# Chunk 0's q and k through two hardware queues, short dummy matmuls, and a new order of the opening

## The chip, the core and the metric

The kernel runs on one core of a Trainium2 chip. The metric is the device time of one execution in microseconds (us), lower is better. The core has five engines that work at the same time and wait for each other by semaphores: TensorE (PE; PEld is its weight load), VectorE (DVE), ScalarE (ACT), GpSimd (POOL) and SyncE (SP). Sixteen DMA engines move data between memory (HBM) and the on-chip buffer (SBUF). Matmul results go to eight PSUM banks, named ps0 to ps7.

## The reference

The kernel computes causal sliding-window attention and passes its result through a gated feed-forward block:

```python
# q, k, v: (8, 8, 576, 64) float32; w_gate, w_val: (512, 1536); w_out: (1536, 512)
scores = q @ k.transpose(0, 1, 3, 2) / 8.0
mask = (rel >= 0) & (rel < 64)              # rel = query position - key position
attn = softmax(where(mask, scores, -1e9))
x = (attn @ v).transpose(0, 2, 1, 3).reshape(4608, 512)
g = x @ w_gate
out = (g * sigmoid(g) * (x @ w_val)) @ w_out    # (4608, 512) float32
```

## The kernel before

The 4608 tokens are cut into 36 chunks of 128 for the attention, and into 9 blocks of 512 (four chunks each) for the feed-forward part. All matmuls are in bf16. Loads from HBM convert float32 to bf16 on their way, and these all are issued by POOL, in one order. SP issues the output DMAs and, for later chunks, DMA transposes.

One chunk n goes through these steps, which are the words of the two tables LOADS and STEPS:

- `kq:n` loads q and k (tiles qn, kn), `v:n` loads v (tile va), `ld:n` does both. `w:a:b` loads columns a to b (in units of 128) of both gate and value weights (Wg, Wv); `wo:a:b` loads rows of the output weights (Wo).
- `TQ:n`, `TK:n` transpose q and k on PE (L293); `qa`, `qd`, `ka`, `kd` move the result from PSUM to qT and kT, on ACT (letter a) or DVE (letter d). `TD:n` does both transposes by DMA on SP instead (L351, L354).
- `S:n` makes the scores on PE (L382), 24 matmuls, and their exponential on ACT (L392, tile pt). It needs kT of chunks n and n-1. Masking is either `M:n`, a multiplication on DVE (L398), or, where `B:n` came before (chunks 0, 2, 3), a bias that PE adds first (L362).
- `A0:n` and `A1:n` are the two halves of pt times v on PE (L432). `N:n` divides by the row sums on DVE (L451, L454, tile xb). `X:n` transposes the result on PE (L529), `xa:n` or `xd:n` moves it to xT; `XD:n` does it by DMA.
- `F:c:f:t0:t1` is one of the 12 parts of the gate and value products of block c, for the columns t0 to t1 (L563): eight matmuls and a tanh on ACT. `U` is the rest of the oldest F on DVE (L572, L574), which writes hT. `O:c:u` is the output product for one chunk (L596), 12 matmuls, a copy on ACT and an output DMA on SP.

The two tables are the order in which every engine gets its instructions: each engine works through its own in that order and waits where data or a buffer is not there yet. Tables cover blocks 0 and 1, most of the attention of chunks 0 to 11, and the scores of 12 and 13. From `F:2:0` on, loops in `build` give the order: per block, 12 F and the four O of the block before, with a pair of chunks placed in the middle of an O (L495, L382). The first such pair is 12, placed in the second O of that loop; it holds `S:14` and `S:15`.

`init` makes constants on DVE: zeros for dummy matmuls (wz), the identity, the masks, and the ones beside v. `warm:10` issues ten dummy matmuls of 512 columns (L318) before any data is there. A PSUM bank goes to the next user that asks, the one that was free longest.

POOL's semaphores come in 16 lanes: a load waits until the 16th load before it has landed. A load into qn or kn also waits until the chunk eight before it has been transposed.

Of the kernel before, what the change touches and what calls it, by code (L numbers as in the profile page):

```python
# [7 lines left out]
B, H, S, D = 8, 8, 576, 64  # L8
DM, DFF = H * D, 1536
T = B * S  # L10
# [8 lines left out]
F32 = dt.float32  # L19
# [130 lines left out]
class _Kernel:  # L150
# [7 lines left out]
    NS = 4  # L158
    NO = 4
    LAST = NFC  # L160
    LOADS = """
    init kq:0 kq:1 kq:2 v:1 v:0 kq:3 v:2 v:3 w:5:7 w:0:2 w:3:5 kq:4 w:7:8 kq:5 v:4 w:2:3 w:10:12 kq:6 w:9:10
    v:6 v:5 w:8:9 kq:7 v:7
    """
    STEPS = """
    warm:10 B:0 TQ:0 qa:0 TK:0 ld:8 ka:0 S:0 TQ:1 TK:1 ld:9 wo:6:12 qd:1 kd:1 TQ:2 qa:2 S:1 TK:2 B:2 kd:2 M:1
    S:2 A0:0 A0:1 A1:0 A1:1 ld:10 N:0 TQ:3 B:3 qa:3 N:1 X:0 TK:3 xa:0 A0:2 ka:3 A1:2 ld:11 wo:0:6 S:3 N:2 X:1
    xd:1 X:2 A0:3 xa:2 A1:3 F:0:5:0:384 N:3 X:3 U F:0:6:0:384 xd:3 F:0:0:0:384 U F:0:1 U U F:0:3 U F:0:4 U
    F:0:7 U TK:4 TQ:4 ld:12 ka:4 TK:5 TQ:5 F:0:0:384:512 qd:4 F:0:5:384:512 U ka:5 S:4 U F:0:2 qd:5 M:4
    F:0:6:384:512 U A0:4 S:5 A1:4 ld:13 U F:0:10 N:4 F:0:11 U M:5 X:4 F:0:9 U xd:4 TK:6 A0:5 U ka:6 A1:5 F:0:8  # L170
    N:5 U X:5 TQ:6 ld:14 xa:5 TQ:7 TK:7 qa:6 F:1:0:0:256 kd:7 qd:7 S:6 F:1:1:0:256 U TQ:8 TK:8 M:6 F:1:2:0:256
    U A0:6 ka:8 U S:7 A1:6 ld:15 TQ:9 N:6 F:1:3:0:256 TK:9 qa:8 U X:6 F:1:4:0:256 xd:6 F:1:5:0:256 U
    F:1:6:0:384 U M:7 ka:9 F:1:7:0:384 U qa:9 A0:7 U S:8 A1:7 ld:16 TQ:10 F:1:8:0:384 N:7 U qa:10 X:7 TK:10
    xa:7 F:1:9:0:384 M:8 ka:10 A0:8 U TD:11 S:9 A1:8 ld:17 F:1:10 N:8 M:9 F:1:11 XD:8 U U A0:9 S:10 A1:9
    F:1:0:256:512 N:9 F:1:1:256:512 U F:1:2:256:512 XD:9 U O:0:0 U M:10 A0:10 S:11 A1:10 O:0:3 N:10 M:11 X:10
    A0:11 xd:10 A1:11 TK:13 N:11 TD:12 TQ:13 ka:13 F:1:3:256:512 qd:13 X:11 F:1:4:256:512 U F:1:5:256:512 U
    TD:14 F:1:6:384:512 U F:1:7:384:512 F:1:8:384:512 U O:0:1 U U xd:11 O:0:2 S:12 S:13 F:1:9:384:512 TD:15
    M:12 U M:13
    """

    def __init__(self, nc, q, k, v, wg, wv, wo, out):
# [5 lines left out]
    def alloc(self):  # L187
        nc = self.nc

        def sb(name, n, dtype=BF):  # L190
            return nc.alloc_sbuf_tensor(name, [128, n], dtype)

        def ring(name, cnt, n, dtype=BF):
            return [sb("%s%d" % (name, i), n, dtype) for i in range(cnt)]

        self.ident = sb("ident", 128)
        self.mask = sb("mask", 128)
        self.Wg = sb("Wg", NK * DFF)[:, :].rearrange("p (c f) -> p c f", c=NK)
        self.Wv = sb("Wv", NK * DFF)[:, :].rearrange("p (c f) -> p c f", c=NK)
        self.Wo = sb("Wo", NF * DM)[:, :].rearrange("p (c m) -> p c m", c=NF)  # L200
        hd = lambda t: t[:, :].rearrange("p (h d) -> p h d", h=H)
        self.qn = [hd(t) for t in ring("qn", self.NQ, DM)]
        self.kn = [hd(t) for t in ring("kn", self.NQ, DM)]
        self.vall = sb("va", self.NV * H * 80)
        va = self.vall[:, :].rearrange("p (i h d) -> p i h d", i=self.NV, h=H)
        self.va = [va[:, i] for i in range(self.NV)]
        self.kT = sb("kT", 4 * (T + 64))[:, :].rearrange("p (c t) -> p c t", c=4)
        self.qa = sb("qT", self.NZ * 4 * 128)[:, :].rearrange("p (c r t) -> p c r t", r=self.NZ, c=4)
        self.qT = [self.qa[:, :, r, :] for r in range(self.NZ)]
        self.one, self.fi, self.df = [sb(x, 128, F32) for x in ("one", "fi", "df")]  # L210
        self.pi = sb("pi", 32, F32)
        self.nmask = sb("nmask", 128)
        self.wz = sb("wz", 512)
        self.pt = [t[:, :].rearrange("p (h x) -> p h x", h=H) for t in ring("pt", self.NP, H * 128)]
        self.rc = ring("rc", 4, 4, F32)
        self.xp = [t[:, :].rearrange("p (j m) -> p j m", j=2) for t in ring("xb", 2, 2 * DM)]
        self.xb = [self.xp[i // 2][:, i % 2] for i in range(4)]
        self.rp = [t[:, :].rearrange("p (j h) -> p j h", j=2) for t in ring("rp", 2, 2 * H, F32)]
        self.xT = [t[:, :].rearrange("p (c t) -> p c t", c=NK) for t in ring("xT", self.NX, NK * 512)]
        self.sig = ring("sig", self.NS, 512)  # L220
        self.uu = ring("uu", self.NS, 512)
        self.hT = [t[:, :].rearrange("p (f t) -> p f t", f=NF) for t in ring("hT", self.NH, NF * 512)]
        self.ost = ring("ost", self.NO, DM, F32)
        self.wup = sb("wup", 1, F32)
        self.ps = [nc.alloc_psum_tensor("ps%d" % i, [128, 512], F32) for i in range(8)]
        self.n_s = 0
        self.pool = {i: i - 8 for i in range(8)}
        self.tb, self.bb, self.ab, self.a1, self.mk, self.glus = {}, {}, {}, {}, {}, []
# [42 lines left out]
    def load_qk(self, n):  # L271
        i = n % self.NQ
        for dst, src, nm in ((self.qn[i], self.q, "qn"), (self.kn[i], self.k, "kn")):
            parts = list(self.segs(128 * n, 128))
            for j, (r, b, s, L) in enumerate(parts):
# [2 lines left out]
                d = dst[r:r + L]  # L278
                self.g.op("pool", lambda e, d=d, a=a: e.dma_start(d, a), writes=ks, dma=True)  # L279

    def move(self, eng, d, a, rk, wk):
        if eng == "act":
            self.g.op("act", lambda e: e.activation(d, a, ACTF.Copy), reads=rk, writes=wk)
        else:
            self.g.op("dve", lambda e: e.tensor_copy(d, a), reads=rk, writes=wk)

    def transposes(self, key, job, reads):
        bank, bk = self.bank()
        tb = bank[:, 0:256].bitcast(BF).rearrange("p (c t) -> p c t", c=4)

        def pe(e):
            for i, a in enumerate(job):
                r = e.transpose(tb[:, i, :], a, self.ident[:, :])  # L293
            return r

        self.g.op("pe", pe, reads=["ident"] + reads, writes=[bk])
        self.tb[key] = tb, bk

    def T(self, which, n):
        t, nm = (self.kn, "kn") if which == "k" else (self.qn, "qn")  # L300
        iq = n % self.NQ
        self.transposes((which, n), [t[iq][:, 2 * c:2 * c + 2, :] for c in range(4)], [(nm, iq, j) for j in range(2)])
# [10 lines left out]
    def warm(self, count):  # L313
        bank, bk = self.ps[7], ("ps", 7)

        def pe(e):
            for _ in range(count):
                r = e.matmul(bank[:, :], self.wz[:, 0:128], self.wz[:, :], start=True, stop=True)  # L318
            return r

        self.g.op("pe", pe, reads=["wz"], writes=[bk])
# [314 lines left out]
    def build(self):  # L636
        W = lambda a, b: (self.load_w("g", a, b), self.load_w("v", a, b))

        def load(n):
# [2 lines left out]
                self.load_v(n)  # L642

        acts = {
            "init": self.init, "v": self.load_v, "w": W, "kq": self.load_qk,
            "wo": self.load_wo, "ld": load,
            "warm": self.warm, "TK": lambda n: self.T("k", n), "TQ": lambda n: self.T("q", n),
            "kd": lambda n: self.ev("k", n, "dve"), "ka": lambda n: self.ev("k", n, "act"),
            "qd": lambda n: self.ev("q", n, "dve"), "qa": lambda n: self.ev("q", n, "act"),
            "B": lambda n: self.bb.__setitem__(n, self.bias(n)),  # L650
# [4 lines left out]
        }  # L655
        for t in (self.LOADS + self.STEPS).split():
            name, *args = t.split(":")
# [15 lines left out]
        pairs = {(2, 1): 12, (2, 2): 14}  # L673
        for n in range(16, NCH, 2):
            pairs[(n - 4) // 4, n % 4] = n
        for c in range(2, self.LAST):
            for u in range(4):
                last = c == NFC - 1 and u == 3
                masks = []
                for s in range(3):  # L680
# [5 lines left out]
                    if s == 1 and not last:  # L686
                        n = pairs.get((c, u))
# [54 lines left out]
```

## Time and profile before

| | us |
|---|---|
| median of 5 runs (lowest to highest) | 336.88 (335.87 to 338.06) |
| the profiled execution, whole time | 336.88 |
| its span, first to last instruction | 335.0 |
| PE busy | 320.6 (96% of the span) |
| DVE busy | 218.0 (65%) |
| ACT busy | 137.4 (41%) |
| POOL busy | 114.5 (34%) |
| first load issued by POOL | 1.25 |
| scores of chunk 0 (S:0) start on PE | 7.53 |
| first F matmul starts | 18.68 |
| first matmul of F:2:0 | 88.94 |

The page cuts the span into 40 slices of 8.4 us. PEclk is the clock that TensorE was granted, in tenths. A row of the chain says from when and for how long the run's last instruction depended on what; "issue" is time in which the engine waited for nothing that the profile shows. Busy PE time includes overlap between matmuls, so the start times of groups are the better clock of its progress.

### The profile page before, as it was taken

How to read it: one execution, taken by the hardware profiler on the slowest of the kernel's cores; microseconds unless marked ns; L12 is line 12 of the kernel's file. 1: busy time of each engine (PE TensorE's matmuls, PEld its weight loads, DVE VectorE, ACT ScalarE, POOL GpSimd, SP SyncE). 2: the span in 40 equal slices, each digit the busy share in tenths (PEclk: the TensorE clock that was granted, in tenths of full speed). 3: DMA queues.
4: the chain of work that ended last, by engine and by line, in shares of the span. 5: the costliest groups of instructions: out<-in, count | busy, mean ns of one | idle time of the engine just before them, and what ended most of it. 6: DMA issues, size and time to landing. Idle time of an engine off the chain costs nothing.

```text
span 335.0 us, 8316 instructions
## 1 busy us (share of the span) xinstructions
PE 320.6 (96%) x3492; PEld 167.0 (50%) x3528; DVE 218.0 (65%) x460; ACT 137.4 (41%) x252; POOL 114.5 (34%) x142
## 2 busy tenths in 40 slices
PE   7799999799899999999999999999999999999997
PEld 3455577467445545454545454545454544444444
DVE  5658999777367766666666666666666666555520
ACT  3634567443525434343525252525252532223222
POOL 8999999590506706050515150100000000000000
PEclk9979999999999999999999999999999999999999
DMA  9999999999999996979696969450506120200012
GB/s 79 157 185 174 166 176 176 159 155 187 174 154 106 142 203 46 158 94 159 94 150 102 180 73 197 51 141 21 139 18 135 25 78 18 78 33 31 32 52 106
DMA packets 168293, 38.56 MB, mean 115 GB/s; under 512 B 157760, under 2 KB 163776, under 8 KB 168256
## 3 DMA queue, kind: packets, MB, share of 16 engines
q0 software_dynamic: 122528, 18.88, 83.2%
q1 hardware_dynamic: 45584, 19.08, 28.7%
q8 instruction: 28, 0.46, 0.5%
q10 hardware_dynamic: 144, 0.07, 0.1%
q14 instruction: 9, 0.07, 0.1%
HBM read 37.75 MB, written 9.44 MB: 141 GB/s over the span
## 4 chain that ended last, share of the span: by engine, by line
PE 86%; DMA 7%; issue 2%; POOL 2%; ACT 1%; DVE 1%; SPq 0%; POOLq 0%
PE ps L563 54%; PE ps L596 24%; DMA va<-in_v_dram 5%; PE ps L382 3%; DMA qT<-qn 3%; PE ps L495 2%; PE ps L432 1%; PE ps L293 1%; POOL qn L279 1%; PE ps L626 1%; POOL kn L279 1%; PE ps L529 1%; SPq L351 0%; ACT pt L392 0%; DVE xb L454 0%
## 5 line engine op out<-in xcount | busy, mean ns | idle before, releaser
L572 DVE SCALAR_TENSOR_TENSOR uu<-sig,ps 128x512 bf16<-128x512 bf16 (+3 forms) x121 | 76.0, 628 | 62.9 <-ACT sig L569 62.4
L563 PE MATMUL ps<-xT,Wv 128*128 128x512 bf16 (+3 forms) x482 | 113.7, 358 | 0.1
L563 PE MATMUL ps<-xT,Wg 128*128 128x512 bf16 (+3 forms) x466 | 110.2, 358 | 1.4 <-issue 0.5
L569 ACT ACTIVATE sig<-ps 128x512 bf16<-128x512 f32 (+3 forms) x121 | 66.7, 552 | 91.9 <-PE ps L563 91.8
L596 PE MATMUL ps<-Wo,hT 128*128 128x512 bf16 x404 | 94.4, 379 | 2.2 <-issue 1.9
L574 DVE SCALAR_TENSOR_TENSOR hT<-uu,ps 128x512 bf16<-128x512 bf16 (+3 forms) x121 | 76.2, 630 | 4.4 <-PE ps L563 0.3
L563 PEld LDWEIGHTS ps<-xT,Wv 128*128 128x128 bf16 x484 | 46.7, 98 | 47.7 <-issue 0.7
L563 PEld LDWEIGHTS ps<-xT,Wg 128*128 128x128 bf16 x484 | 45.7, 98 | 47.8 <-ACT pt L392 1.9
L332 POOL DMA_DIRECT2D va<-in_v_dram x40 | 38.9, 1006 | 82.4 <-PE ps L495 81.3
L596 PEld LDWEIGHTS ps<-Wo,hT 128*128 128x128 bf16 x420 | 40.0, 98 | 46.6
L392 ACT ACTIVATE pt<-ps 128x512 bf16<-128x512 f32 x72 | 37.8, 601 | 26.7 <-PE ps L382 26.5
L608 ACT ACTIVATE ost<-ps 128x512 f32<-128x512 f32 x35 | 20.9, 597 | 66.5 <-PE ps L596 66.4
L279 POOL DMA_DIRECT2D qn<-in_q_dram x40 | 39.1, 996 | 16.4 <-DMA qT<-qn 13.1
L279 POOL DMA_DIRECT2D kn<-in_k_dram x40 | 39.2, 1001 | 0.6 <-DMA qn<-in_q_dram 0.6
L398 DVE TENSOR_TENSOR pt<-pt,mask 128x512 bf16<-128x512 bf16 x66 | 24.3, 419 | 6.3 <-ACT pt L392 6.1
L517 DVE TENSOR_TENSOR xb<-ps,rp 128x448 bf16<-128x448 f32 (+1 forms) x36 | 18.5, 514 | 1.2
L382 PE MATMUL ps<-qT,kT 64*64 64x64 bf16 (+1 forms) x864 | 16.2, 203 | 2.7 <-DMA qT<-qn 1.1
L382 PEld LDWEIGHTS ps<-qT,kT 64*64 64x64 bf16 x864 | 12.5, 108 | 9.2 <-DVE hT L574 4.2
L514 DVE RECIPROCAL rp<-ps 128x7 f32<-128x7 f32 (+1 forms) x36 | 6.7, 187 | 15.4 <-PE ps L495 15.4
L495 PE MATMUL ps<-va,pt 64*64 64x65 bf16 x728 | 11.5, 193 | 0.1
L454 DVE TENSOR_TENSOR xb<-ps,rc 128x256 bf16<-128x256 f32 x24 | 10.2, 425 | 0.8
L432 PE MATMUL ps<-va,pt 64*64 64x65 bf16 x360 | 7.4, 196 | 2.9 <-issue 1.6
(44 smaller groups left out, 97.8 us busy)
## 6 DMA issues: line engine op xcount, KB each, us to landing
out_dram<-ost SPq DMA_DIRECT2D x35, 256.0 KB, 3.3
qn<-in_q_dram POOLq DMA_DIRECT2D x32, 128.0 KB, 7.9
kn<-in_k_dram POOLq DMA_DIRECT2D x32, 128.0 KB, 8.2
va<-in_v_dram POOLq DMA_DIRECT2D x32, 128.0 KB, 7.7
Wo<-in_moe_w_out_dram POOLq DMA_DIRECT2D x2, 768.0 KB, 13.4
Wg<-in_moe_w_gate_dram POOLq DMA_DIRECT2D x4, 256.0 KB, 7.5
Wv<-in_moe_w_val_dram POOLq DMA_DIRECT2D x4, 256.0 KB, 8.1
qn<-in_q_dram POOLq DMA_DIRECT2D x8, 64.0 KB, 7.3
```

Source lines behind the costliest of these rows:

```text
L279: self.g.op("pool", lambda e, d=d, a=a: e.dma_start(d, a), writes=ks, dma=True)
L332: g.op("pool", lambda e, d=d, a=a: e.dma_start(d, a), writes=ks, dma=True)
L382: r = e.matmul(sv[h][o:o + 64, c, q0:q1], self.kT[ps, c, kk:kk + 64], qT[ps, c, q0:q1], start=not biased, stop=not biased or c == 3 and kk ...
L392: g.op("act", lambda e, po=po, si=si: e.activation(po, si, ACTF.Exp, scale=SCALE), reads=[bk], writes=[pk])
L398: "dve", lambda e: e.tensor_tensor(po, po, m, ALU.mult), reads=[pk, "mask"], writes=[pk]))
L517: g.op("dve", lambda e, xo=xo, rb=rb, a=a: e.tensor_tensor(xo, a[:, :, 0:64], rb, ALU.mult), reads=[bk] + rk, writes=wk)
L563: r = e.matmul(bank[:, 0:n], W[:, kk, f * 128:f * 128 + 128], xT[:, kk, t0:t1], start=(kk == 0), stop=(kk == NK - 1))
L569: g.op("act", lambda e: e.activation(sig[:, 0:n], G[:, 0:n], ACTF.Tanh, scale=0.5), reads=[gk], writes=[("sig", i)])
L572: g.op("dve", lambda e: e.scalar_tensor_tensor(uu[:, 0:n], sig[:, 0:n], 1.0, G[:, 0:n], ALU.add, ALU.mult), reads=[("sig", i), gk], writes ...
L574: g.op("dve", lambda e: e.scalar_tensor_tensor(hT[:, f, t0:t1], uu[:, 0:n], 0.5, V[:, 0:n], ALU.mult, ALU.mult), reads=[("uu", i), vk], wr ...
L596: r = e.matmul(OB[:, :], hT[:, f, 128 * u:128 * u + 128], self.Wo[:, f, :], start=(f == 0), stop=(f == NF - 1))
L608: g.op("act", lambda e: e.activation(ost[:, :], OB[:, :], ACTF.Copy), reads=[ok], writes=[("ost", io)])
```

## The change

Chunk 0's q and k no longer come through POOL. `first_load` loads them as float32 by SP (k) and ACT (q), into the two halves of one tile ff, two tokens to a partition. `cast` makes bf16 of it, four heads on ACT and four on DVE; `first_T` transposes each half with four PE transposes, and `first_ev` moves the results to kT and qT. `warm:65` issues dummy matmuls of 64 columns, and wz is smaller. Both tables are new: loads, steps and their splits, which chunks are transposed by DMA (10, 13, 14, 15 instead of 11, 12, 14, 15) and which X go by DMA (10 instead of 8 and 9).

```diff
     LOADS = """
-    init kq:0 kq:1 kq:2 v:1 v:0 kq:3 v:2 v:3 w:5:7 w:0:2 w:3:5 kq:4 w:7:8 kq:5 v:4 w:2:3 w:10:12 kq:6 w:9:10
-    v:6 v:5 w:8:9 kq:7 v:7
+    f:0:1 init kq:1 kq:2 v:0 kq:3 v:1 v:2 v:3 w:7:9 kq:5 kq:4 w:3:4 w:6:7 w:4:5 v:5 w:1:2 v:4 w:9:10 w:2:3 v:6
+    w:5:6 v:7 kq:6 w:0:1 kq:7 w:10:12
     """
     STEPS = """
-    warm:10 B:0 TQ:0 qa:0 TK:0 ld:8 ka:0 S:0 TQ:1 TK:1 ld:9 wo:6:12 qd:1 kd:1 TQ:2 qa:2 S:1 TK:2 B:2 kd:2 M:1
-    S:2 A0:0 A0:1 A1:0 A1:1 ld:10 N:0 TQ:3 B:3 qa:3 N:1 X:0 TK:3 xa:0 A0:2 ka:3 A1:2 ld:11 wo:0:6 S:3 N:2 X:1
-    xd:1 X:2 A0:3 xa:2 A1:3 F:0:5:0:384 N:3 X:3 U F:0:6:0:384 xd:3 F:0:0:0:384 U F:0:1 U U F:0:3 U F:0:4 U
-    F:0:7 U TK:4 TQ:4 ld:12 ka:4 TK:5 TQ:5 F:0:0:384:512 qd:4 F:0:5:384:512 U ka:5 S:4 U F:0:2 qd:5 M:4
...
-    xa:7 F:1:9:0:384 M:8 ka:10 A0:8 U TD:11 S:9 A1:8 ld:17 F:1:10 N:8 M:9 F:1:11 XD:8 U U A0:9 S:10 A1:9
-    F:1:0:256:512 N:9 F:1:1:256:512 U F:1:2:256:512 XD:9 U O:0:0 U M:10 A0:10 S:11 A1:10 O:0:3 N:10 M:11 X:10
-    A0:11 xd:10 A1:11 TK:13 N:11 TD:12 TQ:13 ka:13 F:1:3:256:512 qd:13 X:11 F:1:4:256:512 U F:1:5:256:512 U
-    TD:14 F:1:6:384:512 U F:1:7:384:512 F:1:8:384:512 U O:0:1 U U xd:11 O:0:2 S:12 S:13 F:1:9:384:512 TD:15
-    M:12 U M:13
+    warm:65 ld:8 wo:0:6 B:0 ca:0:0 cd:0:1 T:0:1 T:0:0 ea:0:1 ed:0:0 TQ:1 qa:1 S:0 TK:1 ld:9 kd:1 TQ:2 qa:2 S:1
+    B:2 TK:2 kd:2 A0:0 A1:0 M:1 S:2 TQ:3 N:0 B:3 TK:3 qa:3 kd:3 X:0 A0:1 xa:0 S:3 A1:1 ld:10 A0:2 N:1 A1:2
+    ld:11 A0:3 N:2 A1:3 X:1 xa:1 N:3 X:2 xa:2 X:3 F:0:7:0:384 xd:3 U F:0:8 U TK:5 TQ:5 ka:5 TQ:4 F:0:7:384:512
+    TK:4 ld:12 qa:4 qd:5 ka:4 U F:0:3 U S:4 S:5 F:0:6 M:4 F:0:4 M:5 U F:0:1 U U A0:4 A0:5 A1:4 ld:13 wo:6:12
+    A1:5 F:0:9 N:4 N:5 X:4 F:0:2 U xa:4 X:5 U F:0:5 xd:5 F:1:1:0:128 U TQ:6 F:1:2:0:256 U TK:6 ld:14 qa:6
+    F:1:3:0:256 U F:0:0 kd:6 U U S:6 TK:7 TQ:7 F:1:0:0:256 kd:7 F:0:10 M:6 U qa:7 U A0:6 S:7 A1:6 ld:15 TQ:8
+    TK:8 N:6 F:0:11 M:7 ka:8 qd:8 X:6 A0:7 xa:6 U S:8 A1:7 ld:16 F:1:4:0:384 N:7 F:1:5:0:384 U X:7 U TQ:9 xa:7
+    F:1:6:0:384 M:8 qa:9 TK:9 U F:1:7 kd:9 TD:10 U A0:8 S:9 A1:8 ld:17 F:1:8 N:8 M:9 X:8 TQ:11 xa:8 F:1:9 U
+    qd:11 A0:9 TK:11 U A1:9 ka:11 F:1:10 N:9 TK:12 U X:9 ka:12 TQ:12 F:1:11 xd:9 qd:12 TD:13 S:10 U S:12
+    F:1:1:128:512 M:10 F:1:0:256:512 M:12 A0:10 U S:11 A1:10 U F:1:2:256:512 F:1:3:256:512 N:10 F:1:4:384:512
+    U XD:10 F:1:5:384:512 O:0:0 U U U M:11 O:0:1 A0:11 S:13 A1:11 O:0:2 N:11 M:13 X:11 O:0:3 xd:11
+    F:1:6:384:512 U TD:14 TD:15
     """
...
-        self.wz = sb("wz", 512)
+        self.wz = sb("wz", 128)
...
+    def first_load(self, n, own):
+        for eng, p0, src in (("sp", 0, self.k), ("act" if own else "sp", 64, self.q)):
+            parts = list(self.segs(128 * n, 128))
+            for r, b, s, L in parts:
+                d = self.ff[n][p0 + r // 2:p0 + (r + L) // 2].rearrange("p h j d -> p h (j d)")
+                a = src[b, :, s:s + L, :].rearrange("h (p j) d -> p h (j d)", j=2)
+                self.g.op(eng, lambda e, d=d, a=a: e.dma_start(d, a), writes=[("ff", n, p0 + r)], dma=True)
+
+    def cast(self, n, half, eng):
+        hs = slice(4 * half, 4 * half + 4)
+        d = self.cc[n][:, :, hs].rearrange("p j h d -> p h j d")
+        self.move(eng, d, self.ff[n][:, hs], [("ff", n, p) for p in (0, 64)], [("cc", n, half)])
...
+    def first_T(self, n, half):
+        job = [self.cc[n][:, j, 2 * c:2 * c + 2, :] for c in (2 * half, 2 * half + 1) for j in range(2)]
+        self.transposes(("f", n, half), job, [("cc", n, half)])
+
+    def first_ev(self, n, half, eng):
+        tb, bk = self.tb["f", n, half]
+        cs = slice(2 * half, 2 * half + 2)
+        ta = tb.rearrange("p (c j) (w t) -> p w c t j", j=2, w=2)
+        kd, qd = self.kT[:, cs, 64 + 128 * n:192 + 128 * n], self.qT[n][:, cs]
+        for w, (d, key) in enumerate(((kd, ("kT", n, half)), (qd, ("qT", n, half)))):
+            self.move(eng, d.rearrange("p c (t j) -> p c t j", j=2), ta[:, w], [bk], [key])
+        self.done(bk)
...
-                r = e.matmul(bank[:, :], self.wz[:, 0:128], self.wz[:, :], start=True, stop=True)
+                r = e.matmul(bank[:, 0:64], self.wz[:, :], self.wz[:, 0:64], start=True, stop=True)
```

## The prediction

> **What bounds the kernel now.** I read the head of the page first, then four stretches by windows, then the chain for the first 20 us and for 55 to 90 us, and last the landing times of single loads.
>
> ```profile
> span 335.0 us, 8316 instructions
> ...
> PE 320.6 (96%) x3492; PEld 167.0 (50%) x3528; DVE 218.0 (65%) x460; ACT 137.4 (41%) x252; POOL 114.5 (34%) x142
> ...
> PEclk9979999999999999999999999999999999999999
> ...
> q8 instruction: 28, 0.46, 0.5%
> ```
>
> TensorE is busy 96%; the other 4% and the clock dips in slices 3 and 4 are what an opening can win. The stretches (first matmul of feed-forward block 2 starts at 88.94):
>
> ```profile
> 0.00:5.24 5.24, 4.02 (x10) 1.49 (x11) 4.07 (x17) 1.49 (x2) 4.19 (x9) 1.00 0.66 42
> 5.24:18.68 13.44, 9.30 (x268) 5.93 (x266) 6.57 (x19) 8.20 (x15) 13.44 (x18) 1.00 2.02 157
> 18.68:88.94 70.26, 66.38 (x919) 42.30 (x918) 53.80 (x135) 34.42 (x71) 53.02 (x65) 0.98 2.00 168
> 88.94:335.00 246.06, 240.87 (x2308) 117.26 (x2334) 153.53 (x291) 93.34 (x165) 43.84 (x53) 1.00 0.84 99
> ```
>
> After 88.94 TensorE works without a gap over 0.2 us and its instructions are the same in both kernels (the last 2345 matmuls agree in kind and order), so I keep 246.06 us for it. Everything is decided before 88.94. In the chain:
>
> ```profile
> 7.46 4.42 DMA va<-in_v_dram
> ...
> 15.77 0.71 issue
> ...
> 18.03 0.35 PE ps L432 x16
> ```
>
> ```profile
> 61.06 1.63 issue
> ...
> 78.84 8.55 DMA qT<-qn
> 87.39 0.25 issue
> 87.64 0.70 PE ps L382 x33
> ```
>
> The reader should see three stalls of TensorE: 0.71 us in S:3, 1.63 us in A1:8, and about 1.04 us before S:12 (O:0:2 ends at 86.6, S:12 starts at 87.64), which waits for a DMA transpose of q (TD:12). And the first feed-forward matmuls run at half speed:
>
> ```profile
> 18.68 1.29 PE L563 MATMUL ps<-xT,Wg 128*128 128x384 bf16 x4
> 19.77 1.49 PE L563 MATMUL ps<-xT,Wv 128*128 128x384 bf16 x4
> ...
> 23.19 0.81 PE L563 MATMUL ps<-xT,Wg 128*128 128x384 bf16 x4
> ```
>
> Four such matmuls advance 1.09 to 1.28 us at the granted clock of 0.50 (19 to 22 us), 0.65 us after it. The lost time from 18.68 to 23.19 is 0.44 + 0.63 + 0.21 + 0.41 = 1.7 us. So of the 70.26 us between 18.68 and 88.94, 1.7 + 1.63 + 1.04 = 4.4 are lost. The rest, 65.9 us, is work: 24 F at 8 x 0.216 = 41.4, four O at 2.6 = 10.4, S:4 to S:13 3.7, eight A 4.9, 16 q/k transposes 3.5, seven X 1.5, split F 0.3.
>
> **The change, part by part.**
> *Loads.* POOL issues its first loads every 0.87 us (rows L279). Two leave, so v:0 moves from eighth to fifth: issue at 4.7 instead of 7.46, landing near 9.2 with the same 4.42 us. kq:3 and v:1 to v:3 come 0.9 to 1.8 us earlier. The Trainium skill (DMA: Bandwidth & Descriptors, Issuing engines are not separate DMA queues) speaks against a gain: loads of all engines share the same 16 DMA engines, and another queue saves only the sequencer's issue time, "usually small". The row: in the first 5.24 us the DMA share is 0.66 against 2.02 later, and landings follow each other by 0.85 to 0.9 us, as the issues do; so here issue time is the limit, and I take the gain. By the rule v:0 would land at about 11.9, A0:0 would wait 1.2 us or more, and the sum below would be near 335.5.
>
> *Chunk 0.* New are two hardware-queue loads of 256 KB; nearest row: an output DMA of 256 KB lands in 3.3 us, 6.1 under load. I take 4.2, so 5.0 us. ACT issues q ahead of its table load (1.28 us) and SP has nothing else to do, so nobody waits for these issues. Two casts of 128x512 to bf16 (no row; ACT 128x512 takes 0.60, a DVE copy 0.42 to 0.53; bounds 0.3 and 0.6, I take 0.5). DVE is held by init until 6.08, less 0.15 for the smaller wz: its cast ends at 6.45. The load's lateness hides behind that up to 6 us; beyond, it is on the path. Then 8 transposes (0.45), four half evacuations (two on each engine, 0.3 to 0.38 each): S:0 near 7.8, against 7.53. No gain here; POOL's gain is the point.
>
> *Dummies.* 65 of 64 columns. Cold 128-column transposes follow each other by 0.107 us (21.05 to 21.48), so these lie between 0.053 and 0.107: the burst ends between 4.5 and 6.5. I take 0.08, 5.8 with the clock opening at 5.2. The biases (0.43) still fit before the first transposes at 6.5.
>
> *Chain to the first F*, with durations from the rows: exp S:0 8.3-9.4; qa:2 10.0; exp S:1 11.05; M:1 11.5; exp S:2 12.1; N:0 (1.15 on DVE) 12.65; kd:3 13.05; S:3 13.75; exp S:3 14.9; N:1 15.25, N:2 16.4; A:3 to 15.6; N:3 17.5. The table now puts X:3 ahead of the first F on TensorE, so F:0:7 waits for N:3: 17.8. The end of this chain is DVE, four N of 1.1 us in a row. Add 0.2 for code loading (next point): 18.0 against 18.68, a gain of 0.65. Its weights (11th and 12th load) land at about 15.6 and 17.0: hidden by 1 to 2 us.
>
> *Code loading.* The two "issue" holes lie 626 matmuls apart; with their weight loads and 30 separate waits that is 1282 instructions, five times 256. And 0.46 MB in 28 packets of queue 8 is 16 KB each, 256 instructions of 64 B. The Trainium skill (Runtime: NRT & Kernel Launch, Instruction fetch mechanics) gives the same block of 256 and says that crossing is mostly hidden. Here it is not where 256 instructions pass fast: the 256 instructions ahead of each hole, that hole included, took 5.3 and 6.4 us (from 11.2 to 16.49, 56.3 to 62.69), so I read this as the time a block takes to come. By the rule the holes would be chance and stay (0 gained); by the row, I place the boundaries in the new order. They fall at the start of S:3 (block begun at about 8.0, ready at 13.3 to 14.4, needed at 13.3), in F:0:8 (5.9 us after that one), in A0:5 (11 us), S:6 (10 us), A0:7 (6.3 us), S:9, S:12, and at O:0:0 (6.1 us or more). So A1:8 loses its 1.63 hole, and several near misses remain: I charge 0.4 beside the 0.2 above (bounds 0 and 1.6). Net -1.23.
>
> *Clock.* The stretch 15.6 to 17.8 before F has 12 transposes alone, as sparse as 15.5 to 18.7 before. One cold stretch of 3.4 us is to be expected, part of it before F; F loses 0.5 to 2.8. I take 1.4 instead of 1.7: -0.3.
>
> *Wait for TD:12.* Chunk 12 is now transposed on TensorE (chunks 11 and 12 instead of 10 and 13), so S:12 waits for no DMA: -1.04. TD:13 is issued some 15 us ahead of S:13. But TD:14 and TD:15 stand behind four output DMAs on SP. Issued at 1.3 us each (rows L351, L354), the last goes out near F:2:0 + 6.7; S:15 comes at F:2:0 + 12.9; with the 4.8 us median of qT it is in time, with 8.5 to 9.0 it is up to 2.7 us late. POOL's competing loads of chunk 20 are earlier now, since they no longer wait for TD:12 (13.1 us before). I charge 0.3.
>
> *Weights.* Twenty weight loads on POOL instead of 16, at 0.74 each. Only one pair of double width remains early, so landing follows issue by about 5.7, where 9.2 was reached before. Against first use: Wv 3 lands at 22.1 to 22.6 and is needed at 23.0; W 4 25.0 against 26.4; W 1 27.4 against 28.1; W 10 42.2 against 43.7. Before, margins were about 3 us; now 0.5 to 1.5. I charge 0.3 (bounds 0 and 2).
>
> *Rest.* The two Wo loads move in POOL's queue, the second to behind ld:13: by my count of issues it goes out near 54.4 and, with the 13.4 us of its row, lands at 68, ahead of O:0:0 near 73: nothing, at this cover of 5 us. Eight F parts instead of 13 (0.025 us of TensorE each, one sigmoid and two DVE operations fewer each) gives 0.1; another chunk's X (0.22) on TensorE falls ahead of the first F. DVE is 95% busy from 35 to 45 us before without holding TensorE; a late DVE would show as F waiting for a bank. Charged zero.
>
> Sum: -0.65 - 1.23 - 0.3 - 1.04 + 0.3 + 0.3 = -2.6. The profiled execution took 336.88 (span 335.0 and 1.88 around it), which is also the median of the five: 334.3.
>
> **The rivals.**
> *The waits return elsewhere* (18%). Weights or TD:15 come late by the upper bounds: +1.7 for weights, +2.4 at S:15, not both in full: 336.2 (335.2 to 337.5). For it: the thin margins and q transposes of 8.5 us. Against: the early queue has less double-width backlog.
>
> *The gate does not open* (15%, slower). 65 dummies at 0.053 last 3.5 us, not 4.3, and only 64 columns each; if they count too little, the clock stays at 0.5 until F. TensorE's own work before F is about 7.5 us (32 q/k transposes 1.8, biases 0.9, S 1.5, A 2.4, X 0.9); doubled it adds 7.5, of which half of my 4.9 us of idle absorbs 2.5: F at 22.8, not 17.8, 4.1 after the old start; a second cold window in F adds 0.9; holes and TD:12 still give 1.2 and 1.04 back, and weights are then in time: +2.8, 339.6 (337.5 to 341). It decides when the granted clock is still 0.5 at 8 us. Against: the burst before opened the gate by its end, and it stayed open through a sparse stretch until 18.9.
>
> *Everything falls well* (8%): F starts warm at 17.5, no hole: 332.
>
> *The early queues do nothing* is inside the first rival's lower end (335.5).
>
> **How the numbers follow.** Forecast 59%, 334.3, own range 332.6 to 335.6. What can be told from no change is about 0.5%, 1.7 us: below 335.2 is faster, above 338.6 slower. Faster: 0.54 of the forecast and 0.08: 0.62. Slower: 0.10 of the gate case, 0.04 of the first rival: 0.14. Same: 0.24. The range 332.0 to 338.4 leaves out about 5% below and 14% above.
>
> **What would show it.** Right: first F between 17 and 18.7, F:2:0 between 85 and 87.5; no 1.6 us "issue" hole near 60; no wait of S:12 for qT; v landing near 9.2. Wrong: Wg or Wv rows waiting for a DMA, S:14 or S:15 waiting for qT, a granted clock of 0.5 between 6 and 15 us, or S:0 after 9 us because the chunk 0 loads landed after 6.

## The result, and the profile after

The changed kernel took 334.47 us (median of 42 executions, 331.68 to 335.99) against 336.0 (79 executions) for the kernel before on the same chip: ratio 0.9951, 95% interval 0.9938 to 0.9964. The forecast was 334.3. The size of the gain is another matter: its sum was -2.6, measured against a profiled execution of 336.88 that was slower than the median of the many later executions, and the gain by the ratio is 1.65. The ratios leave out executions in a slower state (of the kernel before 11 of the 45 timed beside the first experiments, near 341 us at a mean granted clock of 0.98 to 0.985; of the kernel after none).

The profiled execution after took 332.87, 1.6 below the median, with a span of 330.9. Its page begins:

```profile
span 330.9 us, 8350 instructions
...
PE 317.8 (96%) x3509; PEld 165.4 (50%) x3547; DVE 216.6 (65%) x453; ACT 137.2 (41%) x249; POOL 115.9 (35%) x144
```

The stretches, cut at the end of the dummies, at the first F and at F:2:0 (length, then busy time and count of PE, PEld, DVE, ACT, POOL, then granted clock, DMA share, GB/s):

```profile
0.00:5.02 5.02, 4.00 (x67) 3.60 (x67) 3.71 (x17) 1.49 (x2) 3.98 (x9) 1.00 0.69 121
5.02:17.71 12.69, 8.74 (x270) 6.00 (x269) 7.97 (x25) 8.79 (x17) 12.69 (x17) 1.00 2.20 163
17.71:84.45 66.74, 63.83 (x868) 38.16 (x877) 52.55 (x125) 34.36 (x68) 58.63 (x72) 1.00 2.06 165
84.45:330.90 246.45, 241.27 (x2312) 117.66 (x2336) 152.36 (x287) 92.56 (x163) 40.63 (x49) 1.00 0.86 101
```

The first F starts at 17.71 instead of 18.68, the middle stretch is 66.74 instead of 70.26, the tail 246.45 instead of 246.06: -0.97 - 3.52 + 0.39 = -4.1, the difference of the two spans. The chain up to the first F:

```profile
0.74 5.05 DMA ff<-in_k_dram
...
5.89 0.44 DVE cc L301
...
14.25 0.42 DVE xb L483
...
17.00 0.44 DVE xb L483
...
17.48 0.40 PE ps L558 x4
17.88 1.30 PE ps L592 x8
```

k of chunk 0 lands after 5.05 us, DVE's cast takes 0.44, and from 14 us on DVE sets the pace with the four N, as forecast; X:3 then releases F. The list of TensorE's waits in the first 100 us (what waited, what ended the wait: us in total, number of waits, the longest) shows neither A1:8 (1.6 before) nor S:12 (1.1 before), and a new one on top:

```profile
PE ps L625 <- DVE uu L601: 1.8, 1, 1.8
PE ps L558 <- DVE xb L483: 1.4, 3, 0.7
```

It stands in front of O:0:0. The timeline there (start, length, instructions, and in brackets the idle time before them and what ended it) shows the weight load beside the matmul:

```profile
70.93 0.10 PEld L625 LDWEIGHTS ps<-Wo,hT 128*128 128x128 bf16 x1
...
72.68 1.39 PEld L625 LDWEIGHTS ps<-Wo,hT 128*128 128x128 bf16 x7 [1.65 <-issue]
...
72.89 1.46 PE L625 MATMUL ps<-Wo,hT 128*128 128x512 bf16 x6 [1.79 <-DVE uu L601]
```

The matmul row names VectorE, which did finish an operation just then. But the weight load, which reads the finished hT of block 0 while VectorE wrote that of block 1, stood still for 1.65 us with "issue". And by a count of TensorE's instructions (matmuls, weight loads and separate waits) it stands at 2241, exactly 512, or two blocks of 256, behind the hole at A1:8 in the kernel before. A boundary, below, is such a place where a new block of 256 begins. Which of the two readings holds was the first question for the experiments.

### The profile page after: what moved, and what is told of

The parts are those of the page before. It is cut to its first block, busy times and chain, and to the rows that moved or that the text cites. A ratio compares the mean times of both kernels' runs of the same rounds, so it can differ in the third digit from the quotient of the medians.

```text
span 330.9 us, 8350 instructions
## 1 busy us (share of the span) xinstructions
PE 317.8 (96%) x3509; PEld 165.4 (50%) x3547; DVE 216.6 (65%) x453; ACT 137.2 (41%) x249; POOL 115.9 (35%) x144
## 4 chain that ended last, share of the span: by engine, by line
PE 93%; DVE 3%; issue 2%; DMA 2%; ACT 0%; DVEq 0%
PE ps L592 56%; PE ps L625 27%; PE ps L411 3%; PE ps L524 2%; PE ps L309 2%; DMA ff<-in_k_dram 2%; PE ps L461 1%; DVE xb L483 1%; PE ps L655 1%; PE ps L558 1%; DVE kT L301 0%; DVE uu L601 0%; DVE rc L480 0%; ACT sig L598 0%; DVE pt L427 0%
## 5 line engine op out<-in xcount | busy, mean ns | idle before, releaser
L601 DVE SCALAR_TENSOR_TENSOR uu<-sig,ps 128x512 bf16<-128x512 bf16 (+3 forms) x116 | 75.2, 649 | 66.6 <-ACT sig L598 66.4
L592 PE MATMUL ps<-xT,Wv 128*128 128x512 bf16 (+3 forms) x462 | 112.2, 364 | 0.1
L592 PE MATMUL ps<-xT,Wg 128*128 128x512 bf16 (+3 forms) x443 | 107.9, 364 | 1.5 <-issue 0.6
L598 ACT ACTIVATE sig<-ps 128x512 bf16<-128x512 f32 (+3 forms) x116 | 65.8, 569 | 87.1 <-PE ps L592 86.9
L603 DVE SCALAR_TENSOR_TENSOR hT<-uu,ps 128x512 bf16<-128x512 bf16 (+3 forms) x116 | 75.4, 650 | 4.0
L361 POOL DMA_DIRECT2D va<-in_v_dram x40 | 39.7, 1014 | 90.1 <-PE ps L524 87.7
L592 PEld LDWEIGHTS ps<-xT,Wv 128*128 128x128 bf16 x464 | 44.7, 98 | 49.0 <-DVE hT L603 0.3
L592 PEld LDWEIGHTS ps<-xT,Wg 128*128 128x128 bf16 x464 | 43.8, 98 | 45.7
L524 PE MATMUL ps<-va,pt 64*64 64x65 bf16 x728 | 11.5, 193 | 0.1
L524 PEld LDWEIGHTS ps<-va,pt 64*64 64x64 bf16 x728 | 9.5, 108 | 0.6 <-DVE hT L603 0.4
```

Of the source, the lines that this page charges most:

```text
L524: r = e.matmul(bb[b][0][ws, 65 * sl:65 * sl + 65], self.pt[(n + j) % self.NP][ks, h, ws], vv[ks, h, 0:65], start=m == q[0], stop=m == q[-1])
L592: r = e.matmul(bank[:, 0:n], W[:, kk, f * 128:f * 128 + 128], xT[:, kk, t0:t1], start=(kk == 0), stop=(kk == NK - 1))
L598: g.op("act", lambda e: e.activation(sig[:, 0:n], G[:, 0:n], ACTF.Tanh, scale=0.5), reads=[gk], writes=[("sig", i)])
L601: g.op("dve", lambda e: e.scalar_tensor_tensor(uu[:, 0:n], sig[:, 0:n], 1.0, G[:, 0:n], ALU.add, ALU.mult), reads=[("sig", i), gk], writes ...
L603: g.op("dve", lambda e: e.scalar_tensor_tensor(hT[:, f, t0:t1], uu[:, 0:n], 0.5, V[:, 0:n], ALU.mult, ALU.mult), reads=[("uu", i), vk], wr ...
```

## The experiments

Each kernel is the one before or the one after with the edit shown; ... stands for the rest of a line or for lines left out. Ratios are to the kernel before, run beside it, with their 95% intervals.

**Is the wait at O:0:0 a late block of code?** *a_fewer* issues 24 TensorE instructions fewer and leaves every dependence alone.

```diff
-    warm:65 ld:8 ...
+    warm:53 ld:8 ...
-    e.matmul(bank[:, 0:64], self.wz[:, :], self.wz[:, 0:64], ...)
+    e.matmul(bank[:, 0:80], self.wz[:, :], self.wz[:, 0:80], ...)
```

> The changed kernel with 53 dummies of 80 columns instead of 65 of 64: the same 4200 columns, but 24 instructions fewer on TensorE, so that the instruction numbered 2241 is no longer the first matmul of O:0:0 but the first of O:0:1, 2.6 us later. Theory A (the 1.8 us wait at O:0:0 is a block of 256 instructions that comes late): the wait goes, or shrinks to under 0.5 us at O:0:1, and the time falls by 1.3 to 1.8 us against the changed kernel, to a median near 332.9. Theory B (O:0:0 waits for VectorE to free a bank of PSUM): the wait stays at O:0:0 with 1.8 us, the time stays within 0.5 us of 334.5.

332.69 us, ratio 0.9909 [0.9882, 0.9936]. In its timeline O:0:0 follows the last F without a wait. (The profiled execution, 335.29, was the slowest of the twelve: TensorE ran at half pace to 13.4 us and again from 20.2 to 23.6, so everything is later.)

```profile
74.98 0.39 PE L592 MATMUL ps<-xT,Wv 128*128 128x128 bf16 x4
75.42 5.13 PE L625 MATMUL ps<-Wo,hT 128*128 128x512 bf16 x23
```

All kernels of this study with the new tables agree: with the boundary at that matmul the wait was 1.79, 1.24, 1.10 and 0.54 us (after, a_fill, a_poolhead, c_after), with the boundary elsewhere none (a_fewer, a_long, a_best, c_poolbest, a_dummy512). The wait belongs to the instruction's number, and the name of VectorE in the row is the releaser that happened to come last. What the wait costs is less than its 1.79 in the first profile: at the same recorded mean clock a_fewer's executions are 1.2 us shorter than those of the kernel after (medians 331.72 against 332.94 at 1.00, 7 and 10 executions). The rest of the 1.8 between the two medians goes with the clock, which was full in more of a_fewer's executions.

The same for the old kernel: *b_shift* is the kernel before with 100 TensorE instructions more.

```diff
-    warm:10 B:0 ...
+    warm:60 B:0 ...
...
-        self.wz = sb("wz", 512)
+        self.wz = sb("wz", 128)
...
-    e.matmul(bank[:, :], self.wz[:, 0:128], self.wz[:, :], ...)
+    e.matmul(bank[:, 0:85], self.wz[:, :], self.wz[:, 0:85], ...)
```

> The kernel before, with one edit: 60 dummy matmuls of 85 columns instead of 10 of 512 (5100 columns against 5120). TensorE gets 100 instructions more ahead of its first real work, so every code block's boundary moves; loads, queues and tables stay as they were. Theory, code loading: the holes of the kernel before at S:3 (0.71 us) and A1:8 (1.63 us) lie at boundaries and go, since the boundaries now stand 5.5 us or more apart; median near 334.0, 2.0 below the kernel before, with no new hole over 0.5. Rival, the holes belong to what the instructions there read: both stay, median 336.

333.84 us, ratio 0.9925 [0.9899, 0.9952]. Both holes are gone; the longest waits of TensorE that are left are ordinary ones:

```profile
PE ps L596 <- issue: 1.9, 12, 0.2
PE ps L432 <- DMA va<-in_v_dram: 1.0, 1, 1.0
```

The wait of S:12 for TD:12 is gone too, with TD:12 where it was in the table: its q went out at 77.36 instead of 78.84 and was there when S:12 came at 85.78 (87.64 before). So that wait hung on about a microsecond of SP's timing. The old kernel with nothing changed but the number and width of its dummies did no worse than the whole change (0.9925 against 0.9951; the intervals overlap).

**What are the two hardware queues worth?** *a_poolhead* is the kernel after with chunk 0 on POOL.

```diff
-    f:0:1 init kq:1 kq:2 v:0 ...
+    init kq:0 kq:1 kq:2 v:0 ...
-    warm:65 ld:8 wo:0:6 B:0 ca:0:0 cd:0:1 T:0:1 T:0:0 ea:0:1 ed:0:0 TQ:1 ...
+    warm:65 B:0 TQ:0 qa:0 TK:0 ld:8 wo:0:6 kd:0 TQ:1 ...
```

> The changed kernel with q and k of chunk 0 by the GpSimd queue as before (kq:0 first, the plain transposes TQ:0 and TK:0), all else as changed. Theory A (the two hardware queues save two issues of 0.87 us, and v:0, kq:3, v:1 land 1.7 us earlier): TK:3 waits for k to about 13.6, S:3 comes 0.8 us later, first F near 18.5 instead of 17.7, median up by 0.8 us to 335.3. Theory B (all queues share the same DMA engines, so nothing is gained): first F within 0.2 us of 17.7, median within 0.3 us of 334.5.

334.90 us, ratio 0.9974 [0.9952, 0.9997]: 0.4 lost by the medians, 0.8 by the ratios, whose intervals overlap. This pair is blurred, since the hole at O:0:0 (1.10 against 1.79) and the clock of the two profiles differ (half pace in a_poolhead from 9.1 to 15.9 us). *b_head* gives the old tables the two queues, with the steps that these need, and nothing else.

```diff
-    init kq:0 kq:1 kq:2 v:1 ...
+    f:0:1 init kq:1 kq:2 v:1 ...
-    warm:10 B:0 TQ:0 qa:0 TK:0 ld:8 ka:0 S:0 ...
+    warm:10 B:0 ca:0:0 cd:0:1 T:0:1 T:0:0 ea:0:1 ed:0:0 ld:8 S:0 ...
```

> The kernel before with the hardware queues' part alone: q and k of chunk 0 by two hardware queues, with their casts, and the table's slots that this needs; 10 dummies of 512 columns as before, so the code blocks' boundaries stay with the instructions they were at. Prediction's sum: the first F comes 0.65 to 0.8 earlier, median near 335.2; by the run with chunk 0 on POOL in the changed kernel, 0.4 to 0.5 earlier, median near 335.6. Rival, the loads' own latency is all that counts: nothing, 336. In each case the holes at S:3 and A1:8 stay within 0.4 of 0.7 and 1.6.

339.75 us, ratio 1.0105 [1.0078, 1.0132]: slower by 3.5, and no theory had that. Its timeline shows why: the same two boundaries, with holes of 1.95 and 2.45 us where the kernel before had 0.70 and 1.63.

```profile
15.44 0.30 PE L412 MATMUL ps<-qT,kT 64*64 64x128 bf16 x9 [0.30 <-ACT kT L300]
17.69 0.52 PE L412 MATMUL ps<-qT,kT 64*64 64x64 bf16 x15 [1.95 <-issue]
...
62.65 0.32 PE L462 MATMUL ps<-va,pt 64*64 64x65 bf16 x15
65.42 0.21 PE L462 MATMUL ps<-va,pt 64*64 64x65 bf16 x1 [2.45 <-issue]
```

The packets that bring these two blocks start at 15.36 and 62.91, 2.3 and 2.5 us ahead of the resumption; in the kernel before they start at 14.0 and 60.06, 2.5 and 2.6 ahead. What differs is how long after the preceding boundary the fetch starts: 2.7 and 3.8 us before, 4.0 and 4.7 here. After the holes the clock fell to half, for 6.8 and 3.4 us, on top (in the kernel before once, for 3.4). *c_headshift* puts b_shift's dummies into b_head, wz with them.

```diff
-    warm:10 B:0 ca:0:0 ...
+    warm:60 B:0 ca:0:0 ...
-    e.matmul(bank[:, :], self.wz[:, 0:128], self.wz[:, :], ...)
+    e.matmul(bank[:, 0:85], self.wz[:, :], self.wz[:, 0:85], ...)
```

> b_head (old tables, chunk 0's q and k by two hardware queues) with b_shift's dummies: 60 of 85 columns, 100 instructions more on TensorE, so every block boundary stands where it stands in b_shift. Theory: b_head lost by the holes at its boundaries alone (1.95 and 2.45 us) and the cold stretches beside them. Then both holes go, and the two queues in the old order are worth what S:3's start shows, nearly nothing: median 333.4 to 334.2, with b_shift's 333.84. Rival, the queues or their casts themselves cost time in the old order: over 336.

332.18 us, ratio 0.9899 [0.9866, 0.9932], 7.6 below b_head with the same loads and tables. Its longest waits between the first F and F:2:0:

```profile
PE ps L593 <- issue: 0.5, 3, 0.2
PE ps L559 <- ACT qT L300: 0.4, 1, 0.4
```

So b_head lost by its boundaries and what followed from them, and the queues are good for more than the "nearly nothing" expected: 1.7 us against b_shift by the medians. (By the ratios 0.9, with intervals that overlap; the two were timed at different times. At a recorded clock of 1.00 the medians are 331.70 and 333.59, of 3 and 5 executions.) In the profiles b_shift waits 1.0 us for v and 0.7 for the first Wg and Wv (its first F starts at 18.93), c_headshift for none of them (18.47, in spite of a clock at half between 8.5 and 12.0). The cleanest pair is *c_poolbest* and a_best (below), which differ as a_poolhead and after do, but have neither a hole nor a clock dip.

```diff
-    f:0:1 init kq:1 kq:2 v:0 ...
+    init kq:0 kq:1 kq:2 v:0 ...
-    warm:47 ld:8 wo:0:6 B:0 ca:0:0 cd:0:1 T:0:1 T:0:0 ea:0:1 ed:0:0 TQ:1 ...
+    warm:47 B:0 TQ:0 qa:0 TK:0 ld:8 wo:0:6 kd:0 TQ:1 ...
```

> a_best with one part undone: chunk 0's q and k come through POOL again (as in a_poolhead). Fillers, dummies and block boundaries are those of a_best, so clock and holes should be equal, and the difference is the worth of the hardware queues in the new order. Prediction: 0.65 to 0.8 of start, 332.4; a_poolhead against the changed kernel at equal clock: 0.4 to 0.5, 332.1. Rival, the queues do nothing: 331.7.

333.48 us, ratio 0.9937 [0.9914, 0.9961], 1.8 above a_best (2.5 by the ratios, whose intervals are apart). First F at 18.67 against 18.02: 0.65, the forecast's figure. Behind it the stretch up to F:2:0 is 0.9 longer, and 0.8 of that is loads that are late:

```profile
PE ps L605 <- issue: 0.6, 4, 0.2
PE ps L309 <- DMA kn<-in_k_dram: 0.5, 1, 0.5
PE ps L605 <- DMA Wv<-in_moe_w_val_dram: 0.3, 1, 0.3
```

(waits between first F and F:2:0). POOL's queue is shorter by two loads for everything behind it, not for v:0 alone.

**The clock.** *c_after* is the changed kernel, unedited, for a second profile.

> The changed kernel once more, unedited, for a second profile. Theory: where the clock has cold stretches they lie before 25 us and lengthen the stretch up to the end of block 0's first F, about 0.4 to 1 us for each 3.4 us; and the wait at O:0:0 is there again, 1.0 to 2.0 us. Rival, that wait was chance in one execution: under 0.3.

333.67 us. In this execution TensorE ran at half pace to about 13.5 us: the eight transposes of chunk 0 took 1.03 us, while those at 13.70 are fast again. In the first profile the eight were fast at once:

```profile
6.37 0.62 PE L309 MATMUL ps<-ident,cc 128*128 128x128 bf16 x8 [0.85 <-DVE cc L301]
```

The rows of c_after:

```profile
6.95 1.03 PE L309 MATMUL ps<-ident,cc 128*128 128x128 bf16 x8 [1.43 <-DVE cc L301]
...
13.70 0.40 PE L309 MATMUL ps<-ident,qn 128*128 128x128 bf16 x4
...
19.87 0.81 PE L592 MATMUL ps<-xT,Wg 128*128 128x384 bf16 x4
...
73.83 5.12 PE L625 MATMUL ps<-Wo,hT 128*128 128x512 bf16 x23 [0.54 <-DVE hT L603]
```

The first F came 2.16 us later than in the first profile, 0.58 of it before the transposes (k landed 0.32 later, its cast took 0.26 longer). The program came only 0.8 later: the wait at O:0:0 shrank by 1.25. TensorE arrived there 2.2 later, the block's packet started only 1.7 later, and from packet to resumption it took 2.4 us instead of 3.2. The granted clock reads 1.00 in the rows of both profiles, since neither trace has a record of it; here the durations of the transposes are the better witness. The Trainium skill (TensorE: Matmul & The Clock Gate, Part 1) says that about 3.4 us of sustained work opens the clock gate, which holds TensorE at half pace until then, in a window that runs freely, so that one kernel shows different numbers of cold matmuls from run to run. The first part, taken alone, is not borne out by this burst: 65 matmuls over 3.65 us, with the two biases right behind them to 5.5 us, opened it by 6.4 us in one execution, and not before 13.5 in the other. The second part fits that, but no run here shows where the window lay.

*a_fill* strews six idle matmuls of 512 columns into the sparse stretch ahead of the first F; `fill:n`, added for it, issues n of them.

```diff
-    ld:11 A0:3 N:2 A1:3 X:1 xa:1 N:3 X:2 xa:2 X:3 F:0:7:0:384 ...
+    ld:11 fill:2 A0:3 N:2 A1:3 X:1 xa:1 N:3 fill:1 X:2 xa:2 fill:3 X:3 F:0:7:0:384 ...
```

With 59 dummies of 70 columns instead of 65 of 64 the boundaries stay.

> The changed kernel with six dummy matmuls of 512 columns in TensorE's gaps ahead of the first F (two before A:3, one before X:2, three before X:3) and six fewer at the start (59 of 70 columns). Theory A (runs of the changed kernel lose time because the sparse stretch before the first F lets the clock fall in most of them, clock 0.99 or 0.995 against 1.0): the clock is 1.0 in nearly all runs, and the median falls by 1.5 us to about 333.0, where the runs at clock 1.0 lie; first F at 17.7 to 18.2. Theory B (the clock falls elsewhere, or the cold time hides behind waits): clocks stay at 0.99 in most runs and the median stays at 334.5, or rises by up to 0.5 for the fillers' own 1.3 us.

333.21 us, ratio 0.9929 [0.9901, 0.9956]. The wait at O:0:0 is still 1.24. The mean granted clock was 0.99 or lower in 26 of 43 executions of the kernel after, in 1 of 8 here. *a_dummy512* goes back to ten dummies of 512 columns in the new tables.

```diff
-    warm:65 ld:8 ...
+    warm:10 ld:8 ...
...
-        self.wz = sb("wz", 128)
+        self.wz = sb("wz", 512)
...
-    e.matmul(bank[:, 0:64], self.wz[:, :], self.wz[:, 0:64], ...)
+    e.matmul(bank[:, :], self.wz[:, 0:128], self.wz[:, :], ...)
```

> The changed kernel with ten dummies of 512 columns as before (110 instructions fewer on TensorE). Theory A (late blocks of 256 instructions): no wait at O:0:0; instead one of 1 to 2.5 us in A:2 near 14.2, since the block that begins there was asked for only 4 us earlier; first F near 18.9, first matmul of F:2:0 within 1 us of the 84.45 of the changed kernel's profile, median 334.0 to 335.0. Theory B (bank wait, and the short dummies matter by themselves): the 1.8 us at O:0:0 stays, first F moves by less than 0.4 us, and the median stays or rises by 0.2 to 0.5 with the longer burst.

333.79 us, ratio 0.9931 [0.9902, 0.996]; no wait at O:0:0, new "issue" holes of 0.80 in A:2 and 0.45 in an F. *a_long* takes a_fewer's number of dummies with 128 columns each.

```diff
-    warm:65 ld:8 ...
+    warm:53 ld:8 ...
-    e.matmul(bank[:, 0:64], self.wz[:, :], self.wz[:, 0:64], ...)
+    e.matmul(bank[:, 0:128], self.wz[:, :], self.wz[:, :], ...)
```

> The changed kernel with 53 dummies of 128 columns instead of 65 of 64: 24 instructions fewer on TensorE (boundaries as in a_fewer, off O:0:0's start), and a burst of 6784 columns, which lasts past the arrival of q and k. Theory, a longer burst keeps the gate open: fewer executions with two cold stretches of 3.4 us, first F not later than 18.6, no wait at O:0:0, median near 332.0. Rival, the burst's length does not matter once it covers one window: clocks as in a_fewer, and the longer burst holds S:0 back by up to 0.5 us: 333.0.

332.93 us, ratio 0.9888 [0.9849, 0.9928], a clock of 1.00 in 3 of 6 executions. It can't be told from a_fewer: a longer burst alone brought nothing that shows.

**All together.** *a_best* has the fillers of a_fill and 47 dummies of 128 columns.

```diff
-    warm:65 ld:8 ...
+    warm:47 ld:8 ...
-    e.matmul(bank[:, 0:64], self.wz[:, :], self.wz[:, 0:64], ...)
+    e.matmul(bank[:, 0:128], self.wz[:, :], self.wz[:, :], ...)
-    ld:11 A0:3 N:2 A1:3 X:1 xa:1 N:3 X:2 xa:2 X:3 F:0:7:0:384 ...
+    ld:11 fill:2 A0:3 N:2 A1:3 X:1 xa:1 N:3 fill:1 X:2 xa:2 fill:3 X:3 F:0:7:0:384 ...
```

> The changed kernel with six 512-column matmuls strewn ahead of the first F as in a_fill, and 47 dummies of 128 columns, which move the boundary of a code block off O:0:0's start. Both gains of the earlier runs together (1.8 for the boundary, 1.3 for the fillers, the latter partly the same executions): median near 331.5, most executions at full clock, no wait over 0.5 at O:0:0. Rival, the two overlap and the fillers' 1.3 us of cold or 0.6 of warm work is paid in full: 332.7, as with the boundary alone.

331.69 us (331.34 to 332.36), ratio 0.9861 [0.9826, 0.9895], better than both kernels; all six executions had a clock of 1.00, and ten of eleven of c_poolbest, which has the same fillers and dummies. Its stretches, cut as above:

```profile
0.00:18.02 18.02, 15.04 (x324) 11.40 (x325) 11.98 (x41) 10.21 (x19) 16.98 (x25) 1.00 1.79 152
18.02:83.03 65.01, 63.83 (x868) 38.10 (x877) 52.56 (x125) 34.37 (x68) 58.02 (x71) 1.00 2.02 165
83.03:329.40 246.37, 241.09 (x2312) 117.24 (x2336) 152.35 (x287) 92.55 (x163) 40.62 (x49) 1.00 0.86 102
```

The middle stretch is 65.01 where the kernel after has 66.74: shorter by 1.73, about the wait at O:0:0 (1.79), with the same 63.83 of TensorE work. The first F comes 0.31 later than in the first profile after, but there chunk 0's transposes start 0.58 later (6.95 against 6.37), so this is not the fillers' price.

## Why the prediction was right, and where it was not

- *Start, -0.65.* Measured -0.97 in that one execution. The chain of DVE's four N ended as drawn (17.8 forecast without a hole, 17.71 measured; S:0 7.84 against 7.8; v:0 issued at 4.88 with 4.6 us of flight, 9.48 against 9.2). The 0.2 charged for a hole at S:3 was not needed. But the execution was an early one. In seven of the other eight profiles with the two queues the transposes of chunk 0 start at 6.94 to 6.96 instead of 6.37: DVE's cast took 0.45 to 0.89 us there and ended at about 6.9 whenever it began, while POOL was issuing a load up to 6.6. That these two hold each other up is a guess. a_best, with the late transposes and the full clock, has its first F at 18.02, a gain of 0.66. By the Trainium skill's rule that another queue saves only issue time, usually little (DMA: Bandwidth & Descriptors, Issuing engines are not separate DMA queues), the gain should have been lost at v:0. It was issue time that was saved, and it was not little: a_best against c_poolbest, 1.8 in all (median).
- *Code loading, -1.23.* The hole at A1:8 went, the mechanism stood, and O:0:0 was among the places named. The size was wrong: 0.4 was charged for all near misses, and O:0:0 alone took 0.54 to 1.79. The step that failed is the price of a near miss: 6.1 us between two boundaries was taken as nearly enough. In the eight holes named so far the fetch starts 2.7 to 5.0 us after the preceding boundary, and TensorE goes on 2.3 to 3.2 later: 5.2 to 8.0 us together (4.5 and 6.1 in the two of a_dummy512). There is no fixed price: in the first profile after, 256 instructions passed from 8.0 to 13.2 us without a hole; there the packet had started at 10.4. The Trainium skill (Runtime: NRT & Kernel Launch, Instruction fetch mechanics) has the blocks right; its "mostly hidden" can fail where 256 TensorE instructions pass in less than these 4.5 to 8.0 us.
- *Clock, -0.3.* In the first profile F lost nothing (its first four matmuls go from 17.71 to 18.36 at full pace), so the credit was too small there. Over many executions it was too large: the mean clock was 0.99 or lower in 26 of 43 executions after, and in 1 of the 34 executions of the kernel before that stood beside the first experiments and count in the ratios, where 0.995 was the commonest value (19). The new tables by themselves are not the reason: with them and without fillers it was 0.99 or lower in 42 of 65 executions with the 64-column dummies (after, a_poolhead), and in 6 of 34 with fewer and wider ones (a_fewer, a_long, a_dummy512). Whether the width of the dummies decides or the boundaries that move with their number, no run separates. The rival "the gate does not open" came true for a part in c_after: half pace to 13.5 us instead of to the F, and the first F at 19.87, 1.2 after the old start instead of 4.1.
- *TD:12, -1.04.* Gone as forecast. But it was gone in b_shift, b_head and c_headshift as well, with the old tables; the move of chunk 12 was not needed for it.
- *TD:14 and TD:15, +0.3, and weights, +0.3.* Neither came: no wait of S:14 or S:15, none for Wg or Wv. Weights landed about 5 us after their issue, where 5.7 was assumed.
- *Rest, 0.* In the middle stretch 1.79 of new wait stands against 1.7 + 1.63 + 1.07 of old ones. That explains 2.6 of the 3.5 gained. The other 0.9 may be work that moved ahead of the first F or fell away with the splits, with 0.39 given back in the tail; these are not separated.

Summed over an execution, the errors nearly cancelled: start, clock of the profiled run and unused charges gave more than forecast, O:0:0 took 1.4 more than was charged. So the forecast hit the median through a right list of causes with two wrong sizes (the near miss and the clock), from a base that was 0.9 too high. From 336.0 the same sum gives 333.4, 1.1 below what was measured: that the forecast lies within 0.2 is in part luck. Two readings in the prediction are off without weight: the clock row dips in slice 3 alone (18.9 to 22.3 us), and the two holes stand 1280 instructions apart by a count in the trace, five times 256 exactly, not 1282.

What the new tables themselves bring can be read where no boundary is in the way. With the two queues, old tables (c_headshift) 0.9899, new ones (a_fewer, a_long) 0.9909 and 0.9888. Without the queues, old tables (b_shift) 0.9925, new ones with fillers (c_poolbest) 0.9937. No difference can be seen. The executions with a recorded clock of 1.00 say it most plainly, though each median has only 3 to 10 of them:

| no hole in the way, clock 1.00 | old tables | new tables |
|---|---|---|
| with the two queues | 331.70 (c_headshift) | 331.72 (a_fewer), 331.78 (a_long), 331.70 (a_best) |
| without them | 333.59 (b_shift) | 333.44 (c_poolbest) |

So the queues bring 1.7 to 1.9 us, the same in both tables, and the order of the opening nothing that shows here. The place of the boundaries is worth 1.2 (a_fewer against after, 331.72 against 332.94) and 1.5 (b_shift against the kernel before run beside it, 333.59 against 335.05; the wait for TD:12 that went along is in it). The whole medians show more, 1.8 and 2.2; their mixes of clocks differ as well.

## What to carry to other kernels

Where TensorE runs through hundreds of short instructions, as here, the number of an instruction can be a cost: mark every 256th, and compare the time between two marks with the 4.5 to 8.0 us that a block took in the holes of these kernels. Some dozens of dummy instructions more or fewer were worth about as much as the two queues, and an order judged by its time alone may only have been lucky with the marks; compare orders at several offsets, and at the same recorded clock. A wait that a row lays on another engine is to be doubted when the weight load beside it says "issue".

## What was not expected of the hardware

- Taking chunk 0's loads off POOL in the old order made the holes larger: b_head lost 1.95 and 2.45 us at the two boundaries where the kernel before lost 0.70 and 1.63. After the preceding boundary the fetch started about 1 us later. What sets this delay stays open; loads in flight at that moment are a guess that no run separates. One program alone shows a spread as well: 1.79 and 0.54 at O:0:0 in the two profiles of the kernel after.
- From the start of a block's packet to the resumption of TensorE it took 2.3 to 2.6 us in seven of eight holes, 3.2 once (at O:0:0 in the first profile), though the packet itself takes about 0.9.
- Filling the sparse stretch held the clock: with fillers and 128-column dummies 16 of 17 executions had a recorded mean clock of 1.00, with the 64-column dummies alone 16 of 65 (after, a_poolhead). Fillers with 70-column dummies gave 4 of 8, wider dummies without fillers 17 of 34 (a_fewer, a_long, a_dummy512), so both seem to be needed; the numbers are small. And a mean of 1.00 is no proof: c_after reads 1.00 too, with TensorE at half pace to 13.5 us.
